# Moving the retention's key scaling from GpSimd to VectorE, and two more weight tiles shifted by ScalarE

## The chip, the core and the metric

The kernel runs on one core of a Trainium2 chip. The metric is the device time of one execution in microseconds (us); the time before is the median of three runs. The engines are named as in the profile: PE is TensorE (PEld its weight loads), DVE is VectorE, ACT is ScalarE, POOL is GpSimd, SP is SyncE, which here only issues transfers. Each engine works through its own instructions strictly in program order and waits for others by semaphores.

## What is computed

A retention layer (linear attention with a decay per head) is followed by two feed-forward layers. B=2, H=8 heads, S=768, D=64; the feed-forward layers have 1536 tokens, width 512 and 2048 hidden units.

```python
for t in range(S):
    state = gamma[None, :, None, None] * state + np.einsum('bhd,bhe->bhde', k[:, :, t], v[:, :, t])
    y[:, :, t] = scale * np.einsum('bhd,bhde->bhe', q[:, :, t], state)
...
x = np.ascontiguousarray(attn_out.transpose(0, 2, 1, 3)).reshape(B * S, H * D)
h = x @ w_in
g = np.maximum(h, 0.0) + np.log1p(np.exp(-np.abs(h)))     # first layer: softplus
x = g @ w_out
h = x @ w_in2
g = h * (1.0 / (1.0 + np.exp(-h)))                        # second layer: silu
return (g @ w_out2).astype(np.float32)
```

The weights arrive as 64-bit floats. The kernel takes each weight apart into a high and a low 32-bit part, and each matrix product is made of three products of such parts.

## The kernel before

The retention is worked off in 12 pieces n = 0 to 11, a chunk of 128 time steps of one of the two batch entries each (n = 2c and 2c+1 are the two entries of chunk c). For a piece there are these steps, each a function with its own line in the profile:

- `att_scores` (PE, L251): 16 products of queries and keys within the chunk, into two banks; `att_mask` (DVE, L259): two multiplications with the decay mask, from PSUM into SBUF.
- `att_within` (PE, L269): 16 products of the masked scores with the values; `att_across` (PE, L291): 32 products of scaled queries with the state of the past, for both pieces of a chunk; these need `att_scale_q` (POOL, L212), one multiplication for each piece.
- `att_split` (ACT L313, with two L311 ahead of it for a piece whose halves lie turned; DVE L314): the result as a high and a low part in `rx`, from which the feed-forward layer reads it.
- `att_scale_k` (L218): one multiplication 128x512 of the keys, in SBUF, by a decay factor for each time step and head (`cs`), into a ring of two buffers. The program calls it for n = 0 to 9. `att_state` (PE, L231): 16 products of these scaled keys with the values, added to the state in PSUM; `att_past` (ACT, L241) copies the state out for the next chunk.

The first layer's work is steps i, each a column block of 128 hidden units for 512 tokens: `gemm1` (PE, L492), `act1` (two softplus on ACT, L511 and L512) and `act2` (DVE, L518, the low part), and later `gemm2` (PE, L532). Before a weight tile u can be used it is converted: `w_exponent` (ACT, L390; where the tile has no shifted copy in memory of its own, ACT also shifts the raw words in place by 16 bits, L394), `w_values` (DVE: L401 and L402 assemble the mantissa from two words where no shifted words are there; L405, L408, L411; L413 takes the mantissa from shifted words with one instruction; L426 writes the low part), `w_split` (ACT, L437, the high part). Some later tiles get the shifted words by a second transfer (`near`), the tiles u = 0 and those of the second layer by L394, and the others of the early ones by L401 and L402.

The order on each engine is that in which the code is written. At the start, the retention's pieces and the first steps of the feed-forward layer are interleaved by hand. On PE it is: scores(0), (1), within(0), (1), state(0), (1), scores(2), (3), within(2), (3), across(2), state(2), (3), gemm1(0), scores(4), (5), gemm1(1), within(4), (5), across(4), scores(6), (7), state(4), (5), gemm1(2), within(6), and so on. The last part of it up to gemm1(0) reads in the code as

```python
        att_split(2)
        att_split(3)
        att_scale_k(2)
        att_scale_k(3)
        att_state(2)
        att_state(3)
        w_exponent(1)
        gemm1(0, 0)
        gemm1(0, 1)
        convert(1)
```

The second layer's weights are combined into seven forms (Strassen's scheme) and come back by transfers; that part is the same in both kernels.

Of the kernel before, what the change touches and what calls it, by code (L numbers as in the profile page):

```python
# [142 lines left out]
def _rows(ap, a):  # L143
    return ap.rearrange("p (a t) -> p a t", a=a)
# [3 lines left out]
def retention_ffn2_kernel(  # L148
# [9 lines left out]
    nc = tc.nc  # L158
# [55 lines left out]
    def att_scale_k(n):  # L214
        c = n // B
        kp = _rows(kp_ring.next(), H)
        kp_t[n] = kp
        nc.gpsimd.tensor_tensor(  # L218
            out=kp,
            in0=a_t[n][:, 3, :].rearrange("p (h d) -> p h d", h=H),  # L220
            in1=cs[:, 8 * c : 8 * c + 8].rearrange("p (h o) -> p h o", o=1).to_broadcast([P, H, D]),
            op=ALU.mult,
        )
# [92 lines left out]
    def att_pair(n):  # L316

        more = n + B < NC
        for b in range(B):
            att_within(n + b)  # L320
        att_across(n)
        for b in range(B):
            att_split(n + b)
        if more:
            for b in range(B):
                att_scale_q(n + B + b)
            for b in range(B):
                att_scores(n + B + b)
            for b in range(B):
                att_state(n + b)  # L330
            att_past()
            for b in range(B):
                att_mask(n + B + b)
            if n + B < NC - B:
                for b in range(B):
                    att_scale_k(n + B + b)
# [3 lines left out]
    tiles = [j for j in jobs if j[0] == "tile"]  # L340
# [17 lines left out]
    def raw(u):  # L358
        return raw_t[u].bitcast(U32).rearrange("p (a b) -> p a b", b=2)
# [27 lines left out]
    def w_exponent(u):  # L387
        z, a = z_ring.next(), a_ring.next()
        conv_t[u] = (a, z)
        nc.scalar.activation(out=z, in_=raw(u)[:, :, 1].bitcast(F32), func=AF.Copy, scale=2.0**-112)  # L390
        if u == 0 or tiles[u][1] == 1:
            near_t[u] = raw(u)[:, :, 0]
            q = raw_t[u].bitcast(U16).rearrange("p (a b) -> p a b", b=4)
            nc.scalar.activation(out=q[:, :, 0:2], in_=q[:, :, 1:3], func=AF.Copy)  # L394
# [360 lines left out]
    def job_start(j):  # L755
        if j[0] == "tile":
            w_exponent(order[j[:4]])
# [61 lines left out]
    with tc.manual_schedule():  # L819
# [29 lines left out]
        att_within(1)  # L849
        att_split(1)  # L850
        att_scale_k(0)
        att_scale_k(1)
        att_state(0)
        att_state(1)
# [12 lines left out]
        att_scale_q(2)  # L867
        att_scale_q(3)
        w_exponent(0)
        convert(0)  # L870
        att_within(2)
# [6 lines left out]
# [5 lines that stand above are left out]
# [26 lines left out]
        for i, n in ((2, 6), (3, 8), (4, 10)):  # L909
            u = order[units[i][0][:4]]  # L910
# [17 lines left out]
        for j in units[5]:  # L928
            u = order[j[:4]]
# [6 lines left out]
        for j in units[6]:  # L936
            u = order[j[:4]]
# [133 lines left out]
```

## Time and profile before

| | |
|---|---|
| time, median of 3 runs | 565.72 us (564.98 to 565.99) |
| time of the profiled execution | 565.84 us |
| its span, first to last instruction | 564.1 us |
| PE busy | 555.2 us (98%) |
| DVE busy | 345.4 us (61%) |
| ACT busy | 295.0 us (52%) |
| POOL busy | 51.7 us (9%) |
| of POOL: L218, ten instructions between 11.06 and 48.54 us | 1035 to 1528 ns each |

The profiled execution lies 1.74 us above its span, and 0.12 us above the median. The busy shares are those of the whole span; the change touches only the first 60 us of it.

### The profile page before, as it was taken

The numbers are of one execution on the slowest core, as the hardware profiler recorded it, in microseconds if no ns is written. First come the engines' busy times: TensorE is split into PE (matmuls) and PEld (weight loads), VectorE is DVE, ScalarE is ACT, GpSimd is POOL, SyncE is SP. The second block draws the span as 40 slices with busy tenths as digits, with TensorE's granted clock in tenths as the row PEclk, the third lists the DMA queues.
The fourth block names the chain that finished last, engine by engine and source line by source line (L and its number), as shares of the span: only waits on it lengthen the run. The fifth ranks groups of instructions, "written<-read, shape, count | busy, mean of one in ns | idle before, by whom it ended". The sixth has DMA issues, their size and how long they took to land.

```text
span 564.1 us, 8150 instructions
## 1 busy us (share of the span) xinstructions
PE 555.2 (98%) x3122; PEld 476.9 (85%) x3122; DVE 345.4 (61%) x608; ACT 295.0 (52%) x533; POOL 51.7 (9%) x64
## 2 busy tenths in 40 slices
PE   7999999999999999999999999999999999999997
PEld 4878888888888888888888889898889999999995
DVE  3996866699998989897944878534432222222112
ACT  1446445676866867786844866435434332332322
POOL 1565000010010111101200011000000000000000
PEclk9999999999999999999999999999999999999999
DMA  8993243398697579857735798764521544444422
GB/s 311 398 412 134 74 153 109 140 335 316 235 362 286 210 247 355 289 195 295 257 163 196 271 390 321 270 250 193 206 74 57 186 186 159 159 161 172 189 76 112
DMA packets 28918, 125.58 MB, mean 223 GB/s; under 512 B 3280, under 2 KB 3280, under 8 KB 25168
## 3 DMA queue, kind: packets, MB, share of 16 engines
q1 hardware_dynamic: 22608, 102.00, 48.9%
q0 software_dynamic: 6272, 23.07, 10.7%
q8 instruction: 24, 0.39, 0.3%
q14 instruction: 14, 0.11, 0.1%
HBM read 98.84 MB, written 26.21 MB: 222 GB/s over the span
## 4 chain that ended last, share of the span: by engine, by line
PE 90%; DVE 5%; DMA 1%; issue 1%; ACT 1%; SPq 0%; POOL 0%; DVEq 0%; POOLq 0%
PE acc L532 23%; PE acc L676 22%; PE h L492 22%; PE by L642 8%; PE bz L642 6%; PE bx L642 6%; DMA cs<-in_cs 1%; PE py L269 1%; PE sc L251 1%; DVE rr L259 1%; PE py L291 1%; PE state L231 1%; DVE rc L408 0%; DVE rc L411 0%; DVE rw L426 0%
## 5 line engine op out<-in xcount | busy, mean ns | idle before, releaser
L492 PE MATMUL h<-rx,rw 128*128 128x512 f32 (+1 forms) x588 | 137.5, 386 | 0.5 <-DVE rw L426 0.5
L532 PE MATMUL acc<-rg,rw 128*128 128x512 f32 x564 | 134.6, 389 | 0.0
L492 PEld LDWEIGHTS h<-rx,rw 128*128 128x128 f32 x588 | 108.5, 188 | 22.7 <-ACT rx L313 0.6
L676 PE MATMUL acc<-rw,rg 128*128 128x512 f32 x477 | 125.3, 391 | 0.0
L532 PEld LDWEIGHTS acc<-rg,rw 128*128 128x128 f32 x564 | 105.7, 188 | 21.6 <-issue 0.2
L676 PEld LDWEIGHTS acc<-rw,rg 128*128 128x128 f32 x477 | 88.5, 188 | 12.6
L661 DVE TENSOR_TENSOR rg<-re,rg 128x384 fp32r<-128x384 f32 x53 | 29.5, 556 | 86.3 <-ACT re L659 86.2
L511 ACT ACTIVATE rg<-h 128x512 fp32r<-128x512 f32 x47 | 27.9, 594 | 62.1 <-PE h L492 49.2
L390 ACT ACTIVATE rc<-rc 128x512 f32<-128x512 f32 x58 | 38.5, 670 | 12.7 <-DMA rc<-in_wts 11.2
L408 DVE SCALAR_TENSOR_TENSOR rc<-rc 128x512 uint32<-128x512 uint32 x58 | 40.9, 705 | 2.0
L658 ACT ACTIVATE rg<-by 128x384 fp32r<-128x384 f32 x16 | 7.9, 492 | 55.8 <-PE by L642 55.8
L731 DVE TENSOR_TENSOR rp<-bz,rp 128x384 f32<-128x384 f32 x16 | 8.9, 558 | 44.1 <-PE bz L642 42.5
L405 DVE TENSOR_SCALAR rc<-rc 128x512 uint32<-128x512 uint32 x64 | 27.1, 423 | 13.3 <-ACT rc L390 13.2
L518 DVE TENSOR_TENSOR rg<-re,rg 128x512 fp32r<-128x512 f32 x47 | 33.0, 703 | 1.7 <-ACT re L512 1.6
L411 DVE TENSOR_SCALAR rc<-rc 128x512 uint32<-128x512 uint32 x64 | 29.1, 455 | 2.2
L642 PE MATMUL by<-f,rw 128*128 128x384 f32 x144 | 29.2, 337 | 0.0
L642 PE MATMUL by<-rx,rw 128*128 128x384 f32 x144 | 29.2, 337 | 0.0
L394 ACT ACTIVATE rc<-rc 128x1024 uint16<-128x1024 uint16 x27 | 28.5, 1055 | 0.0
L512 ACT ACTIVATE re<-h 128x512 f32<-128x512 f32 x48 | 28.4, 593 | 0.0
L642 PEld LDWEIGHTS by<-rx,rw 128*128 128x128 f32 x144 | 25.8, 188 | 2.3 <-ACT by L716 0.4
L437 ACT ACTIVATE rw<-rc 128x512 fp32r<-128x512 f32 x32 | 20.2, 632 | 14.3 <-DVE rc L408 14.3
L642 PEld LDWEIGHTS by<-f,rw 128*128 128x128 f32 x144 | 25.9, 188 | 2.0
(95 smaller groups left out, 703.8 us busy)
## 6 DMA issues: line engine op xcount, KB each, us to landing
rc<-in_wts SPq DMA_DIRECT2D x58, 512.0 KB, 4.6
rw<-d SPq DMA_DIRECT2D x13, 1792.0 KB, 7.4
rw<-d SPq DMA_DIRECT2D x14, 1024.0 KB, 9.2
near<-in_wts SPq DMA_DIRECT2D x21, 511.5 KB, 4.2
d<-st POOLq DMA_DIRECT2D x16, 512.0 KB, 5.6
d<-st POOLq DMA_DIRECT2D x8, 1024.0 KB, 6.1
rp<-in_att SPq DMA_DIRECT2D x10, 512.0 KB, 7.9
d<-w POOLq DMA_DIRECT2D x8, 512.0 KB, 3.7
```

The costliest lines, as they stand in the source:

```text
L390: nc.scalar.activation(out=z, in_=raw(u)[:, :, 1].bitcast(F32), func=AF.Copy, scale=2.0**-112)
L394: nc.scalar.activation(out=q[:, :, 0:2], in_=q[:, :, 1:3], func=AF.Copy)
L408: nc.vector.scalar_tensor_tensor(out=a, in0=hi, scalar=0x80000000, in1=z, op0=ALU.bitwise_and, op1=ALU.bitwise_or)
L411: nc.vector.tensor_scalar(out=z, in0=a, scalar1=0xFF800000, scalar2=None, op0=ALU.bitwise_and)
L492: nc.tensor.matmul(ph[:, t], lhsT=w[:, s], rhs=x[:, kc, t], start=kc == o == j == 0, stop=kc == NPAIR - 1 and j == 2, skip_group_check=i == 0,
L511: nc.scalar.activation(out=ghi, in_=ph, func=AF.Softplus)
L512: nc.scalar.activation(out=t, in_=ph, func=AF.Softplus)
L518: nc.vector.tensor_tensor(out=glo, in0=t, in1=ghi.bitcast(F32), op=ALU.subtract)
L532: nc.tensor.matmul(acc_t[m], lhsT=lhsT, rhs=rhs, start=first and j == 0 and not seeded, stop=last and j == 2, skip_group_check=m in SEEDED,)
L642: nc.tensor.matmul(to, lhsT=a[:, s], rhs=x[:, kc, :], start=start and kc == j == 0, stop=kc == 1 and j == 2, skip_group_check=True,)
L661: rest[c] = lambda: nc.vector.tensor_tensor(out=glo, in0=r, in1=ghi.bitcast(F32), op=ALU.subtract)
L676: nc.tensor.matmul(acc2_t[m], lhsT=a[:, s], rhs=b, start=start and j == 0, stop=stop and j == 2)
```

## The change

`att_scale_k` issues its multiplication on DVE in place of POOL, at the same place of the program. And in `w_exponent` the condition takes in the tiles u = 1 and 2: ACT shifts their raw words in place (L394), and `w_values` then takes their mantissa by L413 in place of L401 and L402. No transfer is added for them.

```diff
         kp_t[n] = kp
-        nc.gpsimd.tensor_tensor(
+        nc.vector.tensor_tensor(
             out=kp,
             in0=a_t[n][:, 3, :].rearrange("p (h d) -> p h d", h=H),
...
         nc.scalar.activation(out=z, in_=raw(u)[:, :, 1].bitcast(F32), func=AF.Copy, scale=2.0**-112)
-        if u == 0 or tiles[u][1] == 1:
+        if u < 3 or tiles[u][1] == 1:
             near_t[u] = raw(u)[:, :, 0]
```

DVE's queue at the first place, behind the splits of pieces 0 and 1 (`py` is the PSUM tile of a piece, `rx` the split result, `sc` the scores):

```order
 L314 TENSOR_TENSOR rx<-py_142,rx 128x4x128
 L314 TENSOR_TENSOR rx<-py_153,rx 128x4x128
+L218 TENSOR_TENSOR rr<-rp,cs 128x512 x2
 L259 TENSOR_TENSOR rr<-sc_0_190,rr 128x512
 L259 TENSOR_TENSOR rr<-sc_1_191,rr 128x512
```

The key scaling of pieces 0 and 1 now stands behind both splits and ahead of the masks of piece 2.

DVE's queue at the second place, behind the splits of pieces 2 and 3 and ahead of the masks of piece 4 (`sc_0_325`); `rc` holds the words of weight tile 1:

```order
 L314 TENSOR_TENSOR rx<-py_224,rx 128x4x128
 L314 TENSOR_TENSOR rx<-py_233,rx 128x4x128
-L401 TENSOR_SCALAR rc<-rc 128x512
-L402 SCALAR_TENSOR_TENSOR rc<-rc 128x512
-L405 TENSOR_SCALAR rc<-rc 128x512
-L408 SCALAR_TENSOR_TENSOR rc<-rc 128x512
-L411 TENSOR_SCALAR rc<-rc 128x512
+L218 TENSOR_TENSOR rr<-rp,cs 128x512
+L218 TENSOR_TENSOR rr<-rr,cs 128x512
+L405 TENSOR_SCALAR rc<-rc 128x512
```

The key scaling of pieces 2 and 3 now stands behind the splits of the same pieces; the two instructions L401 and L402 of tile 1 are gone (an L413 stands further down).

PE's queue at the same place, between across(2) and gemm1(0), with what each instruction waits for:

```order
 L291 MATMUL py_233<-rr 64x128 x2
-L231 MATMUL state<-rp,rr 64x64 [waits Pool_49]
+L231 MATMUL state<-rp,rr 64x64 [waits DVE_49]
 L231 MATMUL state<-rp,rr 64x64 x7
-L231 MATMUL state<-rr 64x64 [waits Pool_49]
+L231 MATMUL state<-rr 64x64 [waits DVE_49]
 L231 MATMUL state<-rr 64x64 x7
```

PE's order is as it was; the state products of pieces 2 and 3 now wait for DVE where they waited for POOL.

## Rows read from the trace of the kernel before

**Rows 1.** The page: the span, and the shares of the chain that ended last.

```profile
span 564.1 us, 8150 instructions
...
PE 90%; DVE 5%; DMA 1%; issue 1%; ACT 1%; SPq 0%; POOL 0%; DVEq 0%; POOLq 0%
```

**Rows 2.** The chain that ended last, 0 to 65 us: start, length, what.

```profile
20.31 1.09 ACT rx L313 x2
...
40.07 2.28 PE py L269 x30
```

**Rows 3.** Timeline of POOL: start, length, instruction, count, idle time before and its releaser.

```profile
11.06 2.04 POOL L218 TENSOR_TENSOR rr<-rp,cs 128x512 f32<-128x512 f32 x2 [10.62 <-DMA cs<-in_cs]
14.14 1.29 POOL L212 TENSOR_TENSOR rr<-rp,rr 128x512 f32<-128x512 f32 x1 [1.04 <-DMA rr<-in_qs]
...
52.52 2.82 POOL L212 TENSOR_TENSOR rr<-rp,rr 128x512 f32<-128x512 f32 x2 [3.99 <-PE py L291]
```

**Rows 4.** Timeline of DVE, 12 to 57 us, in the same columns.

```profile
12.63 0.69 DVE L314 TENSOR_TENSOR rx<-py,rx 128x512 fp32r<-128x512 f32 x1 [0.60 <-ACT rx L313]
...
17.82 1.41 DVE L408 SCALAR_TENSOR_TENSOR rc<-rc 128x512 uint32<-128x512 uint32 x1
19.26 1.15 DVE L411 TENSOR_SCALAR rc<-rc 128x512 uint32<-128x512 uint32 x1
...
28.90 1.27 DVE L401 TENSOR_SCALAR rc<-rc 128x512 uint32<-128x512 uint32 x1
30.20 1.43 DVE L402 SCALAR_TENSOR_TENSOR rc<-rc 128x512 uint32<-128x512 uint32 x1
31.56 0.41 DVE L405 TENSOR_SCALAR rc<-rc 128x512 uint32<-128x512 uint32 x1
...
32.73 1.49 DVE L411 TENSOR_SCALAR rc<-rc 128x512 uint32<-128x512 uint32 x1
34.26 1.66 DVE L426 SCALAR_TENSOR_TENSOR rw<-rc 128x512 fp32r<-128x512 int32 x1
35.84 1.53 DVE L518 TENSOR_TENSOR rg<-re,rg 128x512 fp32r<-128x512 f32 x1
...
38.74 2.47 DVE L259 TENSOR_TENSOR rr<-sc,rr 128x512 f32<-128x512 f32 x4
...
52.25 0.68 DVE L518 TENSOR_TENSOR rg<-re,rg 128x512 fp32r<-128x512 f32 x1
...
54.94 0.95 DVE L314 TENSOR_TENSOR rx<-rr,rx 128x512 fp32r<-128x512 f32 x1 [1.19 <-ACT rx L313]
55.81 2.47 DVE L259 TENSOR_TENSOR rr<-sc,rr 128x512 f32<-128x512 f32 x4
```

**Rows 5.** Timeline of PE, 13 to 60 us, in the same columns.

```profile
13.16 0.69 PE L231 MATMUL state<-rp,rr 128*64 128x64 f32 x16 [0.32 <-POOL rr L218]
...
20.93 0.64 PE L231 MATMUL state<-rr 128*64 128x64 f32 x16
21.53 3.12 PE L492 MATMUL h<-rx,rw 128*128 128x256 f32 x24
...
26.57 3.02 PE L492 MATMUL h<-rx,rw 128*128 128x512 f32 x12
...
36.06 2.97 PE L492 MATMUL h<-rx,rw 128*128 128x512 f32 x12 [0.48 <-DVE rw L426]
...
58.34 1.97 PE L269 MATMUL py<-rr,rp 128*64 128x128 f32 x32
```

**Rows 6.** Timeline of ACT, 15 to 31 us, in the same columns.

```profile
15.97 1.05 ACT L394 ACTIVATE rc<-rc 128x1024 uint16<-128x1024 uint16 x1
...
30.59 0.69 ACT L390 ACTIVATE rc<-rc 128x512 f32<-128x512 f32 x1
```

**Rows 7.** Transfers issued from SP, 32 to 36 us, in the same columns.

```profile
32.76 0.33 SPq L356 DMA_DIRECT2D rc<-in_wts  x1
...
35.19 0.33 SPq L207 DMA_DIRECT2D rr<-in_att  x1
```

## The prediction

> **What bounds the kernel now.** I read the page's chain first: PE holds 90% of it, DVE 5%, POOL nothing [rows 1]. So a change away from PE is worth only what it moves PE's unbroken run. The chain in order of time shows where that run begins: from within(6) at 40.07 us on it is PE to the end, and ahead of that, from ACT's split copies at 20.31 us to 40.07, it is almost all DVE [rows 2]. Between these times lies everything that the change touches but for k8 and k9 (I call the key scaling of piece n "kn" and the query scaling "qn"). I then read the timelines of the four engines there, and from them I work out at what time PE begins gemm1(0), within(6) and within(10) in the changed kernel. Behind within(10) the work is the same in the same order, so what PE has lost or won by then stays to the end.
>
> Two things stand out in the rows. First, a DVE instruction that reads and writes SBUF alone gets longer wherever POOL is at work: L411 takes 1.15 and 1.49 us, L402 1.43, L426 1.66, L518 1.53, where the same L518 takes 0.68 in a quiet place [rows 4]. The masks, which read PSUM, don't: four take 2.47. Second, PE's order is fixed: the state products stand ahead of scores and of gemm1(0), so whoever delivers the scaled keys late holds up all that follows.
>
> **What a moved instruction costs.** No L218 has run on DVE. Both inputs lie in SBUF, so the nearest row is L518, 0.68 us [rows 4]; the lower bound is the 0.41 of the one-input L405, the upper one the 1.66 of L426 beside POOL. I take 0.69. DVE's instructions follow one another more closely than they last: four masks take 2.47, so a follower begins 0.60 after. On POOL the first two took 1.02 each [rows 3].
>
> The GPSIMD Engine Reference of the Trainium skill, section "Engine selection", says that elementwise work on a tile belongs on VectorE, GpSimd being about twice as slow for two inputs. In length the rows bear that out (1.02 against 0.69); taken as a rule for the time it would make this kernel faster, which is the first rival below.
>
> **Place 1, k0 and k1.** On POOL they ended at 13.10 (11.06 + 2.04) [rows 3] and state(1) began at 13.16 [rows 5]. On DVE they stand behind the split of piece 1, which begins at 12.63 [rows 4]: k0 at 13.23, k1 at 13.83 to 14.52. State(1) begins at 14.59, 1.43 later. Scores(2) and (3), their masks, within and across follow in a row on PE and DVE, so ACT's copies of the split of pieces 2 and 3 move from 20.31 to 21.74. POOL's q2, now at 14.14, may wait for k1 by 0.4; its taker across(2) is 4 us away.
>
> What comes back here: L408 and L411 at 17.82 and 19.26 were stretched by 0.72 and 0.74 (to 1.41 and 1.15, against 0.69 and 0.41) by k2 and k3 on POOL. Without that, DVE ends tile 0 as late as before, though its masks came 1.43 later. That is worth nothing here, because DVE then waits for ACT's copies.
>
> **Place 2, k2 and k3: the largest term.** On POOL they were long done when PE had finished across(2); state(3) began at 20.93 and gemm1(0) at 21.53 [rows 5]. That cover is gone. On DVE they stand behind both L314 of the same pieces, and these behind ACT's copies, which now end at 21.74 + 1.09 = 22.83 [rows 2]. The second L314 begins at 22.87, k2 at 23.47, k3 at 24.07 to 24.76. State(3) begins at 24.82, gemm1(0) 0.60 behind it at 25.42: 3.89 us late. Queued behind the waiting state products on PE are gemm1(0) and scores(4), and on DVE the masks of piece 4 wait for these.
>
> **What PE gets back by within(6).** From 21.53 to 40.07 are 18.54 us. PE itself needs from gemm1(0) to gemm1(2) 36.06 - 21.53 less its wait of 0.48, that is 14.05, and 2.97 for gemm1(2) [rows 5]: 17.02. So at most 1.52 comes back, and within(6) begins at 42.44 at the earliest, 2.37 late. Is DVE in time? Gemm1(1) begins 5.04 behind gemm1(0), at 30.46, and ends at 33.48. Before, ACT's L390 of tile 2 began 1.00 behind that end and ended 1.69 behind it [rows 5, 6]; now it ends at 35.17. L405 of tile 2 begins there: L401 and L402, which could run ahead of ACT, are gone, so DVE waits for ACT, a new wait of about 1.2 us (gemm1(0) ends at 28.5; 1.0 for scores(4), half of what lies between gemm1(0) and gemm1(1), 2.4 of masks, 1.2 of k4 and k5 and 0.6 of L518 make 33.8). From L405 to the masks of piece 6 it took 38.74 - 31.56 = 7.18. Of this 1.08 in L411, 0.97 in L426 and 0.85 in L518 was stretch by q6, q7, k6 and k7; L413 adds 0.45. If all that stretch goes, 4.73 remain, the masks begin at 39.9 and the first two end 1.29 later at 41.2, ahead of PE: 2.37 stays the loss. But q6 and q7 stay on POOL; they begin behind across(4), at about 36.4, and meet L411 and its followers again. With two stretches of 0.9 kept, the masks begin at 41.7, the second ends at 43.0 and within(6) is 2.95 late. I take 2.95, as the rows before show the meeting at the same place.
>
> In the SBUF page (SBUF — State Buffer, section "Who interferes with whom") of the Trainium skill the two engines hold a shared pair of ports for a whole instruction, and whoever starts first blocks the other. By that rule k1, too, would block q2, and q6 and q7 cost DVE about one POOL length (1.29) each; the loss at within(6) would be up to 0.6 more. The rows show stretches of 0.7 to 1.1, a POOL length less what had passed of it, so the rule agrees and its price is an upper bound only.
>
> **Place 3, k8 and k9, and tile 3.** k6 and k7 stand behind the masks of piece 7, where DVE had time to spare. k8 and k9 add 1.20 behind the masks of piece 9. Slack there: the first masks of piece 10 ended at 55.81 + 1.27 = 57.08 and within(10) began at 58.34, 1.26 later; DVE also idled 1.19 ahead of 54.94 [rows 4, 5]. This covers 1.20 twice over. But DVE's L426 and L518 of this stretch, done by 52.93 before, slip into q10 and q11, which run 2.82 from 52.52 on [rows 3]: two more stretches of about 1.0. 1.20 + 2.0 - 1.26 - 1.19 = 0.75 as the upper bound, 0 as the lower; I take 0.3.
>
> **Edits at nothing.** ACT's two L394 (1.05 each [rows 6]): the one of tile 1 falls where ACT waits for DVE, that of tile 2 ends at 36.2, ahead of its L413 at 36.9. Uncovered they would be 1.05 each. L401 and L402 with their stretches (1.27 and 1.43 for tile 2) go from a stretch of DVE that now waits for PE or ACT: no gain. Transfers: the load that waits for tile 2's last reader was issued at 32.76, and that of piece 9 stands behind it [rows 7]; they go out some 5 to 6 later, at 39 to 40. PE takes piece 9 only behind within(6) and across(6), after 43.0 + 2.28 = 45.3.
>
> **Sum.** +1.43 and +2.46 at gemm1(0), -0.94 by within(6), +0.3 by within(10): +3.25. Against the profiled execution's 565.84 that is 569.1, against the median of 565.72, 569.0. With the bounds: +2.4 (568.1) to +3.7 (569.4).
>
> **Rivals.**
> - *VectorE's total decides: faster.* If DVE were short of time only in total, what counts is the balance: it sheds 1.46 at tile 0, 2.70 - 0.45 at tile 2, 0.6 at tile 1 (L401 and L402 for an L413) and about 1.0 by k6 and k7, together 5.3, and takes on six times 0.60 = 3.6: 1.7 faster, 564.1. For it speaks that DVE holds the chain from 21 to 40. Against it, that gemm1(0) would have to begin by 23.05 (21.53 + 1.52) for PE to make up its lateness, and ACT's copies alone end at 22.83. Below that point it decides. Chance 0.10.
> - *The lateness is made up: no change.* Gemm1(0) may contain a hidden wait (its second half reads the split of piece 3), and PE might need up to 0.4 less; with k2 quicker than I take it, +1.0 at most, 565.7 to 566.8. Chance 0.13.
> - *Transfers too.* If piece 9's load, issued 5 later, comes when PE is ready for its scores or behind that, PE waits: about 1 to 2 us more, 570 to 571. For it: it is 1 MB behind two others. Against it: DMA has then nothing else. Chance 0.09.
> - *Forecast, as summed.* Chance 0.68.
>
> **How the numbers follow.** About 0.2% (1.1 us) is what a measurement can tell from no change. Faster by more: the first rival, 0.10. Within: 0.13. Slower: 0.68 + 0.09 = 0.77. The range reaches from 566.2, inside the second rival, to 570.4, into the third; it leaves out the first rival and about half of each of the other two. The forecast's own range is 568.1 to 569.4.
>
> **What would show it.** State(3) at 24.8 and gemm1(0) at 25.4 on PE, with a PE wait of 2 to 3 us for DVE's L218 ahead of state(2); L218 at 0.69 on DVE; L408 and L411 of tile 0 at 0.69 and 0.43; DVE waiting for ACT ahead of L405 of tile 2; within(6) at 43.0, within(10) at 61 to 62; all behind it unchanged in length. Wrong it would be if state(2) does not wait for DVE, if L218 lasts over 1 us, or if PE stands idle behind 62 us.

## The result, and the profile after

The changed kernel takes 572.29 us (median of six runs, 569.47 to 575.07) against 565.86 (now the median of six): 1.0117 times as long, interval 1.0081 to 1.0153. The time was forecast at 569.0, in a range of 566.2 to 570.4: the direction came, the size did not. The six runs differ far more among themselves than those before (564.98 to 566.2), and they go with TensorE's mean granted clock, which every run lists:

```
time, us       575.07  574.08  573.73  570.84  569.91  569.47
granted clock   0.990   0.993   0.993   0.997   1.000   1.000
```

The profiled execution is the longest of them, 575.07. Its span, the chain that ended last by engine, and TensorE's clock in 40 slices stand on its page:

```profile
span 573.3 us, 8144 instructions
...
PEclk9789999999999999999999999999999999999999
...
PE 92%; DVE 3%; DMA 2%; ACT 1%; issue 1%; SPq 0%; DVEq 0%
```

The chain holds more of PE and less of DVE than before [rows 1], and the second and third slice, of 14.3 us each, show a clock under full speed. The stretches of the same kernel, with the granted clock as the column behind the busy times (1.00 is 2.4 GHz, 0.50 is 1.2 GHz, the other level; what lies between is a change within the stretch):

```profile
10.00:14.00 4.00, 2.19 (x32) 1.76 (x32) 1.92 (x4) 1.19 (x2) 0.00 (x0) 1.00 1.04 415
14.00:18.00 4.00, 3.54 (x54) 3.41 (x56) 1.22 (x3) 2.10 (x3) 2.77 (x2) 0.71 1.04 394
...
24.00:26.00 2.00, 0.00 (x0) 0.00 (x0) 1.84 (x3) 2.00 (x4) 0.80 (x1) 0.97 1.05 400
26.00:28.00 2.00, 0.94 (x16) 0.94 (x16) 2.00 (x2) 0.11 (x1) 2.00 (x2) 0.50 1.02 396
...
30.00:32.00 2.00, 2.00 (x10) 2.00 (x11) 1.26 (x3) 0.44 (x1) 0.00 (x0) 0.50 1.01 399
...
34.00:36.00 2.00, 2.00 (x34) 1.87 (x33) 0.66 (x2) 1.58 (x3) 0.00 (x0) 1.00 1.05 430
```

The first busy column is PE. It falls silent at the end of the first row and in the third, and at either silence the clock goes to its lower level and stays there for some microseconds, although PE is busy again. Added up over stretches of 1 us, the low level lasts 3.4 us the first time, from 15.7 us on, which is 1.2 us after PE had begun again, and 6.8 us the second time, from 25.9 us on, while PE is still silent. PE's timeline of this kernel tells why it fell silent, and what it then did:

```profile
14.46 1.29 PE L231 MATMUL state<-rp,rr 128*64 128x64 f32 x32 [2.01 <-DVE rr L218]
15.68 2.08 PE L251 MATMUL sc<-rp 64*128 64x128 f32 x16
...
27.06 1.12 PE L231 MATMUL state<-rp,rr 128*64 128x64 f32 x16 [3.37 <-DVE rr L218]
28.76 1.12 PE L231 MATMUL state<-rr 128*64 128x64 f32 x16 [0.58 <-DVE rr L218]
29.82 4.40 PE L492 MATMUL h<-rx,rw 128*128 128x256 f32 x24
...
45.77 3.00 PE L492 MATMUL h<-rx,rw 128*128 128x512 f32 x12 [0.62 <-DVE rw L426]
48.70 2.26 PE L269 MATMUL py<-rr,rp 128*64 128x128 f32 x32
...
66.95 2.60 PE L269 MATMUL py<-rr,rp 128*64 128x128 f32 x32
```

These answer to [rows 5]. PE waits three times for L218 on DVE, 6.0 us in all, where it waited 0.5 for POOL. The scores of piece 2 behind the first wait take 2.08 where they took 1.16, and gemm1(0) behind the second takes 4.40 where it took 3.12. Gemm1(0) begins at 29.82 (before 21.53), within(6) at 48.70 (before 40.07), within(10) at 66.95 (before 58.34). DVE's timeline, answering to [rows 4], and under it POOL's at the same time:

```profile
13.73 1.28 DVE L218 TENSOR_TENSOR rr<-rp,cs 128x512 f32<-128x512 f32 x2
...
21.03 0.69 DVE L408 SCALAR_TENSOR_TENSOR rc<-rc 128x512 uint32<-128x512 uint32 x1
...
25.36 1.65 DVE L218 TENSOR_TENSOR rr<-rp,cs 128x512 f32<-128x512 f32 x1
26.93 1.78 DVE L218 TENSOR_TENSOR rr<-rr,cs 128x512 f32<-128x512 f32 x1
...
40.88 0.43 DVE L405 TENSOR_SCALAR rc<-rc 128x512 uint32<-128x512 uint32 x1 [1.25 <-ACT rc L390]
...
42.41 1.51 DVE L413 TENSOR_SCALAR rc<-rc 128x512 uint32<-128x512 uint32 x1
43.96 1.67 DVE L426 SCALAR_TENSOR_TENSOR rw<-rc 128x512 fp32r<-128x512 int32 x1
...
61.46 1.66 DVE L426 SCALAR_TENSOR_TENSOR rw<-rc 128x512 fp32r<-128x512 int32 x1
63.03 1.78 DVE L518 TENSOR_TENSOR rg<-re,rg 128x512 fp32r<-128x512 f32 x1
```

```profile
25.20 1.26 POOL L212 TENSOR_TENSOR rr<-rr 128x512 f32<-128x512 f32 x1 [7.79 <-DMA rr<-in_qs]
26.42 1.74 POOL L212 TENSOR_TENSOR rr<-rp,rr 128x512 f32<-128x512 f32 x1
```

In a quiet place two L218 take 1.28, as forecast; L408 of tile 0 is back at 0.69. But k2 and k3 come so late here that they meet q4 and q5, which begin when their transfer has landed, at 25.2: they take 1.65 and 1.78 (over 1 us, which the prediction had named as a sign of being wrong). All the other meetings are the forecast ones.

The sum for this execution, place by place, from starts on PE in the two traces. Beside the rows above it uses these, first of the kernel before, then of the changed one:

```profile
13.77 1.16 PE L251 MATMUL sc<-rp 64*128 64x128 f32 x16
...
18.52 1.96 PE L291 MATMUL py<-rr 64*64 64x128 f32 x32
...
24.59 1.16 PE L251 MATMUL sc<-rr 64*128 64x128 f32 x16
```

```profile
21.73 1.96 PE L291 MATMUL py<-rr 64*64 64x128 f32 x32
...
34.15 1.16 PE L251 MATMUL sc<-rr 64*128 64x128 f32 x16
```

Its first transfers land 0.49 later; place 1 costs 1.42 (scores(2) at 15.68 against 13.77, less the 0.49); the low clock in scores and within 1.30 (across(2) is 3.21 late at 21.73); place 2 costs 5.08, of which 0.96 and 1.09 are the stretch of k2 and k3 and 0.5 is state(3) at the low clock; gemm1(0) at the low clock 1.27 more (scores(4) at 34.15 against 24.59); 0.93 comes back by within(6); and within(10) and (11), waiting for masks, last 0.63 longer. Together 9.3; the spans differ by 9.2 (573.3 against 564.1).

### The profile page after: what moved, and what is told of

Read it like the earlier page. It is cut to its first block, busy times and chain, and to the rows that moved or that the text cites. A ratio compares the mean times of both kernels' runs of the same rounds, so it can differ in the third digit from the quotient of the medians.

```text
span 573.3 us, 8144 instructions
## 1 busy us (share of the span) xinstructions
PE 559.4 (98%) x3122; PEld 480.9 (84%) x3122; DVE 349.8 (61%) x616; ACT 297.0 (52%) x535; POOL 39.7 (7%) x54
## 4 chain that ended last, share of the span: by engine, by line
PE 92%; DVE 3%; DMA 2%; ACT 1%; issue 1%; SPq 0%; DVEq 0%
PE h L492 23%; PE acc L532 22%; PE acc L676 22%; PE by L642 8%; PE bz L642 6%; PE bx L642 6%; PE sc L251 2%; PE py L269 2%; DMA rp<-in_att 1%; PE py L291 1%; DMA rw<-d 1%; PE state L231 1%; DVE rr L218 1%; DVE rc L413 0%; DVE rc L408 0%
## 5 line engine op out<-in xcount | busy, mean ns | idle before, releaser
L492 PEld LDWEIGHTS h<-rx,rw 128*128 128x128 f32 x588 | 109.7, 191 | 23.0 <-ACT rx L313 0.7
L676 PEld LDWEIGHTS acc<-rw,rg 128*128 128x128 f32 x477 | 88.5, 188 | 12.6
L408 DVE SCALAR_TENSOR_TENSOR rc<-rc 128x512 uint32<-128x512 uint32 x58 | 40.2, 692 | 2.0
L405 DVE TENSOR_SCALAR rc<-rc 128x512 uint32<-128x512 uint32 x64 | 27.3, 427 | 14.9 <-ACT rc L390 14.9
L394 ACT ACTIVATE rc<-rc 128x1024 uint16<-128x1024 uint16 x29 | 30.6, 1056 | 0.0
L411 DVE TENSOR_SCALAR rc<-rc 128x512 uint32<-128x512 uint32 x64 | 27.3, 427 | 2.2
L642 PEld LDWEIGHTS by<-rx,rw 128*128 128x128 f32 x144 | 25.8, 188 | 2.3 <-ACT by L716 0.4
L642 PEld LDWEIGHTS by<-f,rw 128*128 128x128 f32 x144 | 25.9, 188 | 2.0
```

The source lines that it names most:

```text
L405: nc.vector.tensor_scalar(out=z, in0=z, scalar1=3, scalar2=4, op0=ALU.logical_shift_left, op1=ALU.bitwise_or)
L408: nc.vector.scalar_tensor_tensor(out=a, in0=hi, scalar=0x80000000, in1=z, op0=ALU.bitwise_and, op1=ALU.bitwise_or)
L492: nc.tensor.matmul(ph[:, t], lhsT=w[:, s], rhs=x[:, kc, t], start=kc == o == j == 0, stop=kc == NPAIR - 1 and j == 2, skip_group_check=i == 0,
L642: nc.tensor.matmul(to, lhsT=a[:, s], rhs=x[:, kc, :], start=start and kc == j == 0, stop=kc == 1 and j == 2, skip_group_check=True,)
L676: nc.tensor.matmul(acc2_t[m], lhsT=a[:, s], rhs=b, start=start and j == 0, stop=stop and j == 2)
```

## The experiments

The theory after the result, A: PE's waits for the scaled keys cost 3 to 4 us, and the low clock that follows them costs the rest, differently in each run. The rivals: B, the exchange of L401 and L402 for ACT's L394 and DVE's wait for it; C, VectorE's longer queue as such. Each ratio is to the kernel before, run on the same chip, with its interval. The edits are shown against the changed kernel, but for pieces 0 and 1 alone and pieces 2 and 3 alone, which are shown against the kernel before, and the last two, of which each is shown against the run ahead of it.

**One part at a time.** The first run moves only the key scaling and leaves tiles 1 and 2 as they were:

```diff
-        if u < 3 or tiles[u][1] == 1:
+        if u == 0 or tiles[u][1] == 1:
```

> Only the key scaling moves to DVE; tiles 1 and 2 keep L401 and L402. Theory A (PE waits for the scaled keys on DVE, 3 to 4 us, and the low granted clock that follows PE's gaps costs up to 5.6 more): as the whole change, 569 to 574 us, with the runs spread by their granted clock, and PE waiting 2 to 4 us for L218 ahead of the state products of piece 2. Rival B (the new wait of DVE for ACT's copies of tile 2 and ACT's longer work are the loss): 566 to 567 us.

Measured: 571.24 us, 1.0107 (1.0080 to 1.0135), six runs from 569.35 (clock 1.000) to 575.45 (0.991). Its trace has the first fall of the clock (0.60 from 14 to 18 us) and not the second (1.00 from 22 us on), though PE waits 2.40 us ahead of state(2); k2 and k3 are through there just ahead of q4, which begins at 25.56:

```profile
24.87 0.68 DVE L218 TENSOR_TENSOR rr<-rp,cs 128x512 f32<-128x512 f32 x1
25.47 0.68 DVE L218 TENSOR_TENSOR rr<-rr,cs 128x512 f32<-128x512 f32 x1
```

The second run makes only the other edit, the key scaling being back on POOL:

```diff
-        nc.vector.tensor_tensor(
+        nc.gpsimd.tensor_tensor(
             out=kp,
```

> Only the weight tiles change: tiles 1 and 2 are shifted by ACT, the key scaling stays on POOL. Theory A: no change within 1 us, 565.5 to 566.7, granted clock 1.00 throughout, since DVE's L405 of tile 2 can begin no earlier than ACT's L390 at 31.3, where it began at 31.6. Rival B: most of the loss is here, 569 us or more.

Measured: 566.17, 1.0006 (0.9998 to 1.0015), the clock 0.998 to 1.000. So the loss is the key scaling's, and rival B falls. Nor do the tiles win anything: DVE waits for ACT in the time that L401 and L402 took.

**Holding the clock.** Two products of 128x512 that nobody reads stand on PE ahead of the state products of piece 0, three ahead of those of piece 2 (the trace counts each as two):

```diff
+        fill(2, "fill0")
         att_state(0)
...
+        fill(3, "fill2")
         att_state(2)
         att_state(3)
```

> The whole change, with products that nobody reads put on PE where it waits for the keys: two ahead of the state products of piece 0 and three ahead of those of piece 2, each 128x512, about 0.85 us. Theory A (the waits cost about 3.5 us and the low clock behind them the rest): the granted clock stays at 1.00 or nearly, the median falls from 572.3 to 568.5 to 570 and the runs lie within 1 us of each other. If the low clock comes from something other than PE's gaps, the median stays at 571 to 573 and the runs stay spread. If the clock is no part of the loss, 572 too, at a clock of 1.00.

Measured: 569.96, 1.0077 (1.0065 to 1.0089); five runs from 569.64 to 570.54 at clocks of 0.998 to 1.000. PE has more work and the median is 2.3 us below that without it. The two intervals overlap, because the runs of the changed kernel lie so far apart; but no run with fillers is above 570.54, and four of the six without are. PE's timeline in that run:

```profile
22.73 2.84 PE L846 MATMUL fill<-rr 128*128 128x512 f32 x6
25.51 0.69 PE L231 MATMUL state<-rp,rr 128*64 128x64 f32 x16
26.02 0.64 PE L231 MATMUL state<-rr 128*64 128x64 f32 x16
26.59 3.14 PE L492 MATMUL h<-rx,rw 128*128 128x256 f32 x24
...
44.20 2.26 PE L269 MATMUL py<-rr,rp 128*64 128x128 f32 x32
...
62.45 2.60 PE L269 MATMUL py<-rr,rp 128*64 128x128 f32 x32
```

Gemm1(0) takes 3.14, as before the change. Here 4.1 of the loss are left, at full clock. That is a little more than the waits cost alone: k3, from 25.07 on, would have let state(3) begin some 0.2 earlier, so the second filler is too long by that. The two runs of the changed kernel at a clock of 1.000 lost 3.6 and 4.05.

**Which wait brings which fall.** The same with the first filler only, and with the second only:

> The whole change with products that nobody reads at the first place only (two ahead of the state products of piece 0). If the two falls of the clock come each from the wait ahead of it: the clock stays at full speed from 15 to 19 us, falls behind 26 in some runs; 569.5 to 573 us, spread. If the second fall needs the first: as with both fillers, 569.5 to 570.5.

> The whole change with products that nobody reads at the second place only (three ahead of the state products of piece 2). If each wait brings its own fall of the clock: it falls at 15 to 19 us in most runs and not behind 26; 570 to 572 us. If the filler at the second place is enough: 569.5 to 570.5.

Measured: 570.89 (1.0080, 1.0067 to 1.0093) and 570.86 (1.0082, 1.0069 to 1.0094), from 569.6 at clocks of 0.998 to 1.000 up to 571.2 and 571.5 at 0.996. The stretches of the run with the first filler, and then of that with the second:

```profile
15.00:19.00 4.00, 3.78 (x60) 3.11 (x57) 2.68 (x5) 2.12 (x3) 1.84 (x2) 1.00 1.04 395
...
25.00:29.00 4.00, 4.00 (x33) 3.93 (x32) 3.90 (x5) 0.63 (x1) 2.88 (x2) 0.59 1.05 406
```

```profile
15.00:19.00 4.00, 4.00 (x44) 3.71 (x42) 1.52 (x3) 2.10 (x3) 1.78 (x2) 0.57 1.05 399
...
25.00:29.00 4.00, 4.00 (x52) 3.17 (x51) 3.97 (x4) 0.52 (x1) 3.25 (x2) 1.00 1.05 405
```

Each wait brings its own fall, and its own filler keeps the clock up. With one of them left, the runs at clocks of 0.996 and 0.997 take 1.1 to 1.9 us more than those at 0.998 to 1.000; so not every run has a fall.

**Two pieces only.** Keys of pieces 0 and 1 alone on DVE (the tiles as before):

```diff
-        nc.gpsimd.tensor_tensor(
+        (nc.gpsimd if n > 1 else nc.vector).tensor_tensor(
             out=kp,
```

> Only the keys of pieces 0 and 1 are scaled by DVE; tiles 1 and 2 as before. Theory A: PE waits about 2 us ahead of the state products of piece 0, the low clock follows at 15 to 19 us in most runs, and what is lost is partly made up by within(6): 566 to 568 us, with a spread of up to 2 us that goes with the granted clock. If the loss hangs on pieces 2 and 3 alone: 565.8 us.

Measured: 568.75, 1.0060 (1.0039 to 1.0082), in heaps: six runs at 567.1 to 567.65 with a clock of 1.000, one at 569.85 (0.996), five at 571.6 to 571.8 (0.992). The expected spread of up to 2 us was too small; the profiled execution, one of the last, shows how it comes about (none of the six at full clock was traced):

```profile
13.98 1.39 PE L231 MATMUL state<-rp,rr 128*64 128x64 f32 x32 [2.01 <-DVE rr L218]
15.30 2.08 PE L251 MATMUL sc<-rp 64*128 64x128 f32 x16
...
31.91 4.58 PE L492 MATMUL h<-rx,rw 128*128 128x512 f32 x12 [2.57 <-DVE rw L426]
```

The first fall makes PE late, DVE's work on tile 1 then meets POOL's q4, q5, k4 and k5 and is late in turn, PE waits 2.57 for it, and the clock falls again: gemm1(1) takes 4.58 for 3.02. The counterpart, pieces 2 and 3 alone (the condition is `n not in (2, 3)`):

> Only the keys of pieces 2 and 3 are scaled by DVE; tiles 1 and 2 as before. Theory A: PE waits some 2.5 to 3 us for L218 ahead of the state products of piece 2; 1 to 1.5 us of it come back by within(6); at a clock of 1.00 567 to 568.5 us, and runs 2 to 5 us above that where the granted clock falls behind the wait. If the clock falls only behind the first wait (pieces 0 and 1): all runs within 1 us of each other.

Measured: 567.55, 1.0036 (1.0025 to 1.0048): four runs at 567.2 to 567.6 (clock 0.999 to 1.000), two at 568.9 and 569.1 (0.997), 1.4 to 1.6 above them where 2 to 5 were expected. The clock falls behind the second wait alone, too. PE's timeline of one of the latter:

```profile
23.15 0.69 PE L231 MATMUL state<-rp,rr 128*64 128x64 f32 x16 [2.40 <-DVE rr L218]
...
24.41 4.55 PE L492 MATMUL h<-rx,rw 128*128 128x256 f32 x24
```

At full clock each of the two places costs some 1.6 us by the end of the kernel (medians of the runs at full clock, 567.3 and 567.5, against 565.7 and 565.9).

**All but these four on DVE.** The whole change, with k0 to k3 on POOL (`n < 4`):

> The whole change, but the keys of pieces 0 to 3 are scaled by POOL again; those of pieces 4 to 9 by DVE. Theory A: no PE wait for L218 over 0.5 us, clock 1.00, 565.3 to 566.5 us. Rival C (any key scaling on DVE costs its own length): 567 us or more.

Measured: 565.69, 0.9997 (0.9989 to 1.0006), clock 0.998 to 1.000. Six of the ten key scalings on DVE cost nothing by the end, though DVE waits 1.24 for ACT there too: rival C falls as the cause of the loss, place decides. It is a balance, though: within(10) lasts 2.54 here where it took 1.97, which fits the forecast price of k8 and k9 on DVE, and PE had come to across(6) 0.9 earlier than before.

**Other work for PE in the waits.** The first try moved the state products only:

```diff
-        att_state(0)
-        att_state(1)
-        att_past()
...
         att_scores(3)
         att_mask(3)
+        att_state(0)
+        att_state(1)
+        att_past()
```

and those of pieces 2 and 3 behind the masks of piece 5 in the same way.

> The whole change, with the state products of pieces 0 and 1 moved behind the scores of piece 3, and those of pieces 2 and 3 behind the scores of piece 5, so that PE has other work while DVE scales the keys. Theory A: the waits ahead of both go, the granted clock stays at 1.00, 565.5 to 567.5 us, with a rest of up to 1 us from DVE's wait for ACT at tile 2. Rival B (L394 and ACT's copies): 568 us or more. Rival C (VectorE's longer queue itself is the loss, wherever the state products stand): 568 to 570 us at a clock of 1.00.

Measured: 583.49, 1.0314 (1.0301 to 1.0328). This was no test of the theories: in the program the products now stood behind transfers that overwrite the values of pieces 0 and 2, so the state was summed from other pieces' values, and PE waited 12.6 us for those transfers. For the next run the masks and scores went ahead of these transfers as well:

```diff
         att_scale_k(0)
         att_scale_k(1)
+        att_scores(2)
+        att_mask(2)
+        att_scores(3)
+        att_mask(3)
         att_state(0)
         att_state(1)
         att_past()
         att_load(5, 0, 2)
...
         att_scale_k(2)
         att_scale_k(3)
-        att_state(2)
-        att_state(3)
         w_exponent(1)
         gemm1(0, 0)
         gemm1(0, 1)
         convert(1)
         act1(0)
+        att_scale_q(4)
+        att_scale_q(5)
+        att_scores(4)
+        att_mask(4)
+        att_scores(5)
+        att_mask(5)
+        att_state(2)
+        att_state(3)
         att_past()
         qs_load(3)
```

> The whole change, with the state products of pieces 0 and 1 behind the scores of piece 3 and those of pieces 2 and 3 behind the scores of piece 5 on PE; the transfers that overwrite what these products read stand behind them again. Theory A (PE's waits for the scaled keys, and the low clock behind them, are the whole loss): no PE wait of over 0.5 us for L218, granted clock 1.00, within(6) about 39.0 against 40.1 before, 564.5 to 566 us. Rival B (DVE's wait for ACT's copies of tile 2 is the loss): 567 to 569. Rival C (VectorE's longer queue itself is the loss, wherever PE's products stand): 568 to 570 at a clock of 1.00.

Measured: 565.47, 0.9995 (0.9986 to 1.0003), all runs at clocks of 0.999 or 1.000. PE's timeline:

```profile
15.15 1.15 PE L231 MATMUL state<-rp,rr 128*64 128x64 f32 x32
...
20.49 3.45 PE L492 MATMUL h<-rx,rw 128*128 128x256 f32 x24
...
25.86 0.69 PE L231 MATMUL state<-rp,rr 128*64 128x64 f32 x16
...
39.47 2.29 PE L269 MATMUL py<-rr,rp 128*64 128x128 f32 x32
...
57.74 2.62 PE L269 MATMUL py<-rr,rp 128*64 128x128 f32 x32
```

No state product waits any more, and the whole loss is gone with all ten scalings on DVE. Two things are left. Within(10) lasts 2.62 (1.97 before), the price of place 3 again, and PE has won as much by across(6), which begins at 41.70 (before 42.28); whether k8 and k9 on POOL would gain the 0.6 was not tried. And DVE waits for ACT at tile 2, 1.38 here. The next run takes this wait away too: ACT copies tile 2 ahead of the softplus of step 1.

```diff
+        w_exponent(2)
         first(1)
         act2(0)
-        w_exponent(2)
```

> As the run with late state products, and ACT makes its two copies of tile 2 ahead of the softplus of step 1, so that DVE need not wait for them. If DVE's wait for ACT costs anything once PE's waits are gone, up to 0.6 us less than that run: 564 to 565.5 us; if PE's own work decides by then, the same.

Measured: 564.98, 0.9985 (0.9977 to 0.9994): 0.7 us faster than the kernel before. Its DVE goes through without a wait there, within(10) is back at 1.97, and PE has a new wait, for the load of piece 9:

```profile
29.91 0.41 DVE L405 TENSOR_SCALAR rc<-rc 128x512 uint32<-128x512 uint32 x1
```

```profile
38.33 1.97 PE L269 MATMUL py<-rr,rp 128*64 128x128 f32 x32
...
43.40 1.16 PE L251 MATMUL sc<-rr 64*128 64x128 f32 x16 [0.98 <-DMA rr<-in_att]
```

The last run puts the state products of pieces 4 and 5 ahead of the scores of pieces 6 and 7, since that load overwrites piece 4.

```diff
+            if n == B * 2:
+                for b in range(B):
+                    att_state(n + b)
+                att_past()
             for b in range(B):
                 att_scores(n + B + b)
-            for b in range(B):
-                att_state(n + b)
-            att_past()
+            if n > B * 2:
+                for b in range(B):
+                    att_state(n + b)
+                att_past()
```

> As the run with late state products and early copies of tile 2, and the state products of pieces 4 and 5 stand ahead of the scores of pieces 6 and 7, so that the load of piece 9, which overwrites piece 4, can be issued about 1.5 us earlier; PE waited 0.98 us for it. If that wait is the next bound: 0.5 to 1 us less than that run, 564.0 to 564.6. If something else comes in its place: 564.7 to 565.3.

Measured: 564.89, 0.9984 (0.9975 to 0.9992), the same as without it. PE still waits 0.83 for that load:

```profile
43.29 1.16 PE L251 MATMUL sc<-rr 64*128 64x128 f32 x16 [0.83 <-DMA rr<-in_att]
```

The load is issued at 33.08 where it was issued at 35.02, 1.9 earlier, and the wait is only 0.15 shorter. The transfers are busy all the time from 33 to 40 us (share 1.03), so the load seems held by the transfers ahead of it and not by its issue; that was not tested further.

## Why the prediction was wrong

**The step that failed** is the pricing of PE's waits, in "Place 1", "Place 2" and "What PE gets back by within(6)": they took all that PE does behind a wait at the durations of the rows before, all of them at a granted clock of 1.00, and no rival had PE slower. The trace of before had no gap like the two new ones (behind PE's start its longest wait is 0.6 us), so it could not show what follows one. With 2.0 and 3.4 us of silence in the profiled execution the clock stood at 1.2 GHz for 3.4 and 6.8 us. The clock is about 2.3 us of the 6.4 lost in the median (572.29 without, 569.96 with the fillers), and some 3.1 of the 5.6 by which the longest run exceeds the shortest (575.07 against 569.47; 1.30, 0.5 and 1.27 in the sum above). That left the median above the range.

In the Trainium skill, TensorE: Matmul & The Clock Gate, section "HAM oscillation — how this bites in real kernels", idle gaps of PE throw the clock to its lower level, and the work behind them starts slow. The traces here agree in kind, and the fillers show it from the other side; but the waits that the section describes last 3 to 5 us, and here waits of 2.0 and 2.4 us were followed by a fall in part of the runs.

**A second part of it** hangs on the first. K2 began at 25.36 where 23.47 was forecast, 1.30 of it from the clock and 0.49 from the first transfers of that execution. So k2 and k3 reached the time of q4 and q5 and were stretched to 1.65 and 1.78. That time hardly moves: q4 begins between 25.1 and 25.8 us in every trace here but that of the misplaced loads, and in most the profile names the landing of its transfer as what released it. The clock alone did not bring the meeting: in the run with the keys alone, with the same first fall and transfers that landed earlier, k3 began 0.09 ahead of q4 and lasted 0.68. The prediction had k3 done at 24.76, and where the first fall was absent it was: with the first filler state(3) begins at 24.84 (24.82 forecast).

**The steps that held.** L218 costs 0.69 on DVE beside nothing; POOL's 1.02 is 1.5 times that, less than the factor of about two that the prediction quotes and calls borne out. Place 1 cost 1.42 (1.43). 0.93 came back by within(6) (0.94), though there the agreement is in part luck: PE had already waited 0.62 ahead of gemm1(2) for the stretched L426, a wait that the prediction did not have, and gemm1(2) and the masks that it did have ended within 0.1 us of each other. DVE waits 1.25 for ACT at tile 2 (1.2), q6 and q7 stretch two instructions of tile 2 by 1.1 and 1.0 (0.9 each), L408 of tile 0 is back at 0.69 without use. (Two whole POOL lengths, 2 x 1.29, would be 0.8 above 2 x 0.9, not the 0.6 that the prediction gives.) Place 3 cost 0.63 at within(10) and (11), where 0.3 was taken of 0 to 0.75. The runs at a clock of 1.000 took 569.47 and 569.91, 0.5 and 0.9 us above the 569.0 for the likeliest case, inside the range. That the loss sits in place 1 and place 2, and not in the tiles or in DVE's total, the runs with single parts show.

**The rivals.** "VectorE's total decides" fell: with the same total and the state products later the time is that of before or 0.7 us less, and with them in place it is 6 us more. "The lateness is made up" fell too: even at a clock of 1.000 the changed kernel lost 3.6 and 4.05. "Transfers too" didn't come in the changed kernel; the load of piece 9 is waited for only once PE is early.

**Left open:** why one run has a fall and the next, of the same program, has none. No run here tells it.

## What to carry to other kernels

Where a change makes TensorE wait, price the wait at its length and, as a case of its own, at its length plus the work behind it at half the clock; and look what that lateness runs into next, here POOL's query scalings, which a transfer's landing releases. A helper engine that seems slower may be the right one, because its result is ready before the consumer asks: moved to the end of a busy engine's queue, a shorter instruction arrives later. When runs of one kernel spread more than before, set their times against their granted clocks before looking for anything else; and the wait of a strictly ordered engine was cured here by the order (other ready work ahead of it), with the producer left as it was.

## What the hardware showed that was not expected

A silence of 2.0 us on PE, at 12.5 to 14.5 us, was followed by a fall of the clock in some of the runs; so was the wait of 2.57 us ahead of gemm1(1). The wait of 2.40 us ahead of state(2) was followed by one in the traces of pieces 2 and 3 alone and of the first filler, and by none in that of the keys alone. Products on PE that nobody reads lowered the median (572.29 to 569.96). And the runs with keys 0 and 1 alone come in heaps 4.4 us apart, of the same program; the one difference on record between the heaps is the granted clock (0.992 against 1.000).
